# Inverse-step units in the transform's last slots, a penalty placed later, and fewer constant products

## The chip, the cores and the metric

The kernel runs on one core of a Trainium2 chip. The metric is the device time of one execution in microseconds, taken as the median of several runs. Before the change it is 1426.28 us (three runs, 1420.32 to 1427.12 us).

## The reference

A Fourier filter along the sequence, and then a layer of eight experts with a fixed capacity. Each token goes to its best expert that still has room, the tokens being served in the order of their largest scores; 19,968 tokens, 2,496 places per expert.

```python
def _attn_ref(x, filt_r, filt_i):              # x: (8, 2496, 256)
    X = np.fft.rfft(x, axis=1)
    Y = X * (filt_r + 1j * filt_i)[None]
    return np.fft.irfft(Y, n=x.shape[1], axis=1).astype(np.float32)

def _moe_ref(x, w_gate, w1, w2):               # N, D, E, F = 19968, 256, 8, 1024
    logits = x @ w_gate
    order = np.argsort(-logits.flatten())
    for idx in order:
        tok, e = int(idx) // E, int(idx) % E
        if assigned[tok] >= 0 or counts[e] >= N // E:
            continue
        assigned[tok] = e
        counts[e] += 1
    for e in range(E):
        h = np.maximum(x[assigned == e] @ w1[e], 0.0)
        out[assigned == e] = h @ w2[e]
```

## The kernel before, in words

**Transform.** The class Fft works through the eight batches in slots, ten to a batch: a list of events in run(), each with a slot and a priority, is sorted and emitted in that order, and a scheduler then arranges the instructions of each engine. Per batch there are two forward steps (s1, s2), the filter, transposes (tr, line 246) and a first inverse step (inv1, line 291), whose result goes to the tensor zd in DRAM. The scores of the gate are taken in the frequency domain: gate products (line 257), a copy of their sums (line 259), a transpose back (trv, line 282), and inverse steps of their own (v1, v2, v3, lines 326 to 353).

**Last inverse step.** It is cut into 40 units, five to a batch (inv2, lines 390 to 413). A unit loads a tile z from zd (line 375, SP's queue), multiplies it by the constant cD on TensorE in up to three products (line 408), copies each product from PSUM (line 409, ScalarE here) and stores the rows to the tensor xs (line 412). A unit has five columns and three products (512, 512 and 256 wide), the fifth of each batch two columns and one product. The units of the last six batches are the list rest, 30 of them, numbered from 0. The table FILL (line 28) gives the slots, counted from the end of the transform, in which its first units run, each followed by the load of the unit 15 places on, into a buffer that comes free. The others run behind the transform, and the last seven of them store from SP's queue.

**Routing.** The class Route serves the experts in eight phases. Phase 0 finds, in eleven rounds, a threshold for the expert that fills up first: VectorE compares the scores with candidates (Gm, line 587), TensorE counts (line 595, then line 608 over the partitions), VectorE picks the next candidates. At the end it has the members; places() turns them into row numbers, chunk by chunk of 512 rows (lines 787 to 810; xid at line 803 are the rows to gather). Line 755 adds a penalty to the scores of the full expert before phase 1 looks at them again (reduction at line 672, equality and multiplication at 674 and 676, reduction at 678, the assignment matrix A at 682).

**The seam.** Behind the transform, TensorE's order is written by hand: the generator after() hands out the rest of the units product by product, and the class Pump places the steps of the routing between them, by a clock of its own to which each piece of TensorE work adds its length. When the row numbers of the first chunk stand in the program, the remaining units are emitted, and after them 36 constant products (line 1051), whose result nobody reads. POOL then issues the load of the first expert's first weight (line 834) behind the copy of the last unit, four gathers of rows from xs (line 853), and the load of the second weight. The gathers wait for the row numbers and for all stores to xs.

**Experts.** The class Ffn transposes the gathered rows (turn, line 867; copies at 870 and 871), multiplies by the first weight (line 888) and by the second (lines 946 and 948), adds the halves on POOL (line 959) and scatters rows to the output (line 960). The weights are split into a high and a low part (split, copy on ScalarE at line 846, difference on VectorE at line 847). The routing of the next phase runs beside each expert, its counts in TensorE's queue between the expert's products.

Of the kernel before, what the change touches and what calls it, by code (L numbers as in the profile page):

```python
# [9 lines left out]
AF, OP, AX = mybir.ActivationFunctionType, mybir.AluOpType, mybir.AxisListType  # L10
# [6 lines left out]
S = B * G  # L17
# [7 lines left out]
ORD, TF = (1, 0, 0, 1), (3, 5)  # L25
ORD2 = [(0, f) for f in range(6)] + [(1, f) for f in range(4)] + [(0, 6), (0, 7)] + [(1, f) for f in range(4, 8)]
I1, EZ = 5, 0.8
FILL = (-1.5, 0.0, 1.5)
V1, V1D, V2, V3, VP, I2, AC = 8, 0.5, 3, 2, -1, 5, 6.5
NP, NZ, MZ, NXO, ZB, NH = 6, 4, 8, 4, 2, 10  # L30

# [89 lines left out]
class Fft:  # L121
# [293 lines left out]
    def run(s, cp, wp, xp, ps, freed, prep, rest):  # L415
# [51 lines left out]
        for u in rest[NZ:NZ+3]:  # L467
            at(10*B - min(3, I2 - 5.6), 9, s.load_z, *u)
        for k, o in enumerate(FILL):
            at(10*B + o, 5, s.inv2, *rest[k])  # L470
# [17 lines left out]
class Route:  # L488
# [176 lines left out]
    def phase(s, ph):  # L665

        nc = s.nc
# [29 lines left out]
        if ph < 7:  # L697
# [22 lines left out]
            with s.tc.issue_after(x.ins):  # L720
                expert()
                nc.vector.tensor_tensor_scan(cum, s.one[:117], eqm, 0.0, op0=OP.mult, op1=OP.add)
                pen = v("pen", [128, 8])
# [28 lines left out]
        if ph == 7:  # L752
            return
        if ph == 0:
            nc.vector.tensor_tensor(s.lg, s.lg, pen[:117].unsqueeze(1).to_broadcast([117, S, 8]), op=OP.add)
        for e in range(8 if ph else 0):
            nc.scalar.activation(s.lg[:, :, e], s.lg[:, :, e], AF.Identity, bias=pen[:117, e:e+1], scale=1.0)  # L757
        with s.tc.issue_after(s.last):
# [212 lines left out]
def emit(tc, i, out):  # L971
    nc = tc.nc
    with ExitStack() as st:
# [29 lines left out]
        def after():  # L1003
            nonlocal W
            q = 5
            for k in range(len(FILL), len(rest)):
                if k == 3 + NZ + MZ:
# [34 lines left out]
        with tc.manual_schedule(engines={mybir.EngineType.PE}):  # L1042
            while (0, 0) not in pump.tags:
                pump.feed(0.1)
                c = next(units, None)
                pump.feed(c if c else 0.8)
            for c in units:
                pass
            p = ps.tile([128, 512], F32, name="rest", tag="b", bufs=2)
            for _ in range(36):  # L1050
                nc.tensor.matmul(p, R.ones16[:117], R.iota, start=True, stop=True)

        zst.close()
# [135 lines left out]
```

## Time and profile before

| | |
|---|---|
| median of three runs | 1426.28 us |
| profiled execution | 1427.79 us |
| its span | 1426.0 us |
| TensorE busy | 1375.7 us, 96% |
| VectorE busy | 938.6 us, 66% |
| ScalarE busy | 715.8 us, 50% |
| POOL busy | 656.2 us, 46% |
| granted TensorE clock, mean | 0.987 |

The rows below come from this one profiled execution. PE is TensorE, DVE is VectorE, ACT is ScalarE, SP is the engine that only issues transfers. Times count from the start of the span. In a timeline a row is a start, a length, the engine and the line, with the number of records (one fp32 product is two records) and, in brackets, how long the engine sat idle before it and what ended that. Products are pipelined, so that the lengths of neighbours overlap.

### The profile page before, as it was taken

Reading aid. Unit: us, or ns where it says so; the run is one execution under the profiler, and the core shown is the slowest. Engines: PE = TensorE matmul, PEld = TensorE weight load, DVE = VectorE, ACT = ScalarE, POOL = GpSimd, SP = SyncE. Lnnn points to the kernel's source line nnn. Section 1 sums busy time; section 2 is a strip of 40 time slices with the busy share of each in tenths; the row PEclk is TensorE's granted clock in tenths of the full one; section 3 lists DMA queues with packets and bytes.
Section 4 is the critical chain, followed back from the end, with each engine's and each line's share of the span. In section 5 each row is a group of like instructions: output and inputs, shape, how many; then the busy total and the mean of one; then the engine's idle time right before and its main releaser. Section 6 shows DMA issues by size and latency. Waiting matters only on the chain.

```text
span 1426.0 us, 24833 instructions
## 1 busy us (share of the span) xinstructions
PE 1375.7 (96%) x9139; PEld 1142.4 (80%) x9139; DVE 938.6 (66%) x2575; ACT 715.8 (50%) x1644; POOL 656.2 (46%) x724
## 2 busy tenths in 40 slices
PE   8999999998988999999999999999999999999998
PEld 7999998776547788877887877787788788888887
DVE  6776766584686797668668768877867845333231
ACT  6777776444553464354436435534533645433332
POOL 6344443241025556554554653646536454445423
PEclk9999999998989999999999999999999999999999
DMA  9455556878961122121112112112101321111100
GB/s 357 152 166 159 159 154 174 245 266 272 345 253 56 33 96 62 32 85 49 51 36 90 54 45 84 52 43 95 45 27 54 131 71 47 41 47 54 40 23 28
DMA packets 55389, 152.37 MB, mean 107 GB/s; under 512 B 9356, under 2 KB 29964, under 8 KB 51172
## 3 DMA queue, kind: packets, MB, share of 16 engines
q0 software_dynamic: 17552, 57.72, 12.3%
q1 hardware_dynamic: 11357, 53.88, 10.4%
q10 hardware_dynamic: 26359, 39.19, 9.2%
q8 instruction: 72, 1.18, 0.3%
q14 instruction: 49, 0.40, 0.1%
HBM read 87.08 MB, written 63.70 MB: 106 GB/s over the span
## 4 chain that ended last, share of the span: by engine, by line
PE 58%; DVE 7%; ACT 2%; issue 2%; DMA 0%; POOL 0%; POOLq 0%; DVEq 0%; ACTq 0%
PE pz L888 26%; PE py L946 18%; PE py L948 9%; PE ptr L867 2%; PE rt L595 2%; DVE hl L902 1%; ACT lg L757 1%; PE py L938 1%; PE rt L795 1%; DVE OH L789 1%; DVE Gm L587 1%; ACT junka L800 1%; DVE X L605 0%; DVE z L871 0%; DMA xg<-xs,xid 0%
## 5 line engine op out<-in xcount | busy, mean ns | idle before, releaser
L946 PE MATMUL py<-w,hl 128*128 128x512 f32 x1216 | 336.4, 397 | 3.1 <-ACT y L958 3.1
L894 ACT ACTIVATE hl<-pz 128x512 fp32r<-128x512 f32 (+1 forms) x320 | 187.7, 588 | 222.2 <-PE pz L888 193.0
L959 POOL TENSOR_TENSOR y<-y 128x256 f32<-128x256 f32 x152 | 128.9, 850 | 309.0 <-ACT y L958 308.1
L888 PE MATMUL pz<-xo,w0h 128*128 128x512 f32 (+1 forms) x640 | 259.6, 406 | 8.7 <-DVE z L871 3.2
L888 PE MATMUL pz<-xo,w0l 128*128 128x512 f32 (+1 forms) x640 | 254.9, 398 | 0.0
L902 DVE SCALAR_TENSOR_TENSOR hl<-pz,hl 128x512 fp32r<-128x512 f32 x233 | 159.1, 686 | 123.0 <-ACT hl L894 110.3
L946 PEld LDWEIGHTS py<-w,hl 128*128 128x128 f32 x1216 | 210.3, 189 | 31.3 <-ACT y L958 3.5
L853 POOL DMA_INDIRECT xg<-xs,xid x160 | 167.0, 1044 | 107.3 <-issue 35.7
L958 ACT COPY y<-py 128x512 f32<-128x512 f32 x152 | 88.7, 586 | 248.3 <-PE py L948 178.2
L948 PEld LDWEIGHTS py<-w,hl 128*128 128x128 f32 x1216 | 185.6, 188 | 24.7 <-DVE hl L902 0.7
L948 PE MATMUL py<-w,hl 128*128 128x256 f32 x1216 | 200.1, 284 | 0.3 <-DVE hl L902 0.2
L888 PE MATMUL pz<-z,w0h 128*128 128x512 f32 (+1 forms) x640 | 196.6, 388 | 0.0
L960 POOL DMA_INDIRECT out<-y,oid x160 | 171.4, 1071 | 45.5 <-POOL y L959 34.7
L888 PEld LDWEIGHTS pz<-xo,w0h 128*128 128x128 f32 x640 | 121.8, 190 | 32.0 <-DVE z L871 3.9
L888 PEld LDWEIGHTS pz<-z,w0h 128*128 128x128 f32 x640 | 121.4, 190 | 21.7 <-DVE z L871 0.2
L219 ACT COPY Y<-p 64x240 f32<-64x240 f32 (+1 forms) x304 | 116.2, 382 | 41.6 <-PE p L212 20.3
L888 PEld LDWEIGHTS pz<-xo,w0l 128*128 128x128 f32 x640 | 122.3, 191 | 15.5
L235 POOL TENSOR_TENSOR P<-P 128x256 f32<-128x256 f32 x80 | 58.7, 734 | 163.2 <-DVE P L233 162.1
L587 DVE TENSOR_TENSOR Gm<-M,thr 117x1232 bf16<-117x1232 f32 (+2 forms) x80 | 104.4, 1315 | 0.2
L212 PE MATMUL p<-cS,xr 117*128 117x120 f32 x688 | 97.5, 281 | 2.3 <-DMA xr<-xl 2.3
L212 PEld LDWEIGHTS p<-cS,xr 117*128 117x128 f32 x688 | 89.3, 198 | 5.3 <-DMA xr<-xl 2.5
L227 PE MATMUL p<-cW,Y 128*128 128x128 f32 x640 | 88.1, 277 | 1.8 <-ACT Y L219 1.8
(233 smaller groups left out, 2228.7 us busy)
## 6 DMA issues: line engine op xcount, KB each, us to landing
zd<-zt ACTq DMA_DIRECT2D x80, 256.0 KB
xr<-xl SPq DMA_DIRECT2D x6, 1536.0 KB
z<-zd SPq DMA_DIRECT2D x14, 640.0 KB
xr<-xl SPq DMA_DIRECT2D x7, 1216.0 KB
xs<-xo ACTq DMA_DIRECT2D x13, 600.0 KB
xr<-zd SPq DMA_DIRECT2D x8, 640.0 KB
xs<-xr ACTq DMA_DIRECT2D x8, 600.0 KB
xs<-Y ACTq DMA_DIRECT2D x6, 600.0 KB
```

Source lines behind the costliest of these rows:

```text
L212: nc.tensor.matmul(p[:, q-q0, :120], s.xr[b][:117, q], s.cS1, start=True, stop=True)
L219: x = (nc.vector.tensor_copy if dve else nc.scalar.copy)(dst, src)
L587: nc.vector.tensor_tensor(Gm[:, s0:s1, :m], s.M[:, s0:s1].unsqueeze(2).to_broadcast([117, s1 - s0, m]), thr[:117].unsqueeze(1).to_broadcas ...
L853: s.lastg = s.nc.gpsimd.indirect_dma_start(out=xg[:n], out_offset=None, in_=s.xs, in_offset=bass.IndirectOffsetOnAxis(ap=ids[0][:n, t:t+1] ...
L888: nc.tensor.matmul(p[:, :n], w[:, sl], x[:, k, :n], start=m == 0, stop=m == 5)
L894: s.lasta = nc.scalar.activation(h[:, :n], p[:, :n], AF.Relu).ins
L902: nc.vector.scalar_tensor_tensor(l[:, :n], p[:, :n], 0.0, h[:, :n].bitcast(F32), op0=OP.max, op1=OP.subtract)
L946: nc.tensor.matmul(pp, hs[g][f][:, hi], w2[:, :, 256*f:256*f+256], start=m == 0, stop=False, skip_group_check=True)
L948: nc.tensor.matmul(pp[:, f % 2], hs[g][f][:, lo], w2h[:, 256*f:256*f+256], start=False, stop=m > 13, skip_group_check=True)
L958: s.lasta = nc.scalar.copy(yy, pp).ins
L959: nc.gpsimd.tensor_tensor(y, y, yy[:, 1], op=OP.add)
L960: st = nc.gpsimd.indirect_dma_start(out=out_rows, out_offset=bass.IndirectOffsetOnAxis(ap=ids[1][:w, 4*g+t:4*g+t+1], axis=0), in_=y[:w], i ...
```

## The change

It has three parts. FILL gets five entries instead of three: the first five units of the list run in the last slots of the transform, units 3 and 4 being new there, with the loads of units 18 and 19. The penalty of phase 0 is to be issued behind the instruction that Route.last names, the first chunk's row numbers. Of the constant products there are 32 instead of 36.

```diff
@@ -25,7 +25,7 @@
-FILL = (-1.5, 0.0, 1.5)
+FILL = (-3.0, -1.9, -0.8, 0.3, 1.4)
@@ -752,7 +752,8 @@
         if ph == 0:
-            nc.vector.tensor_tensor(s.lg, s.lg, pen[:117].unsqueeze(1).to_broadcast([117, S, 8]), op=OP.add)
+            with s.tc.issue_after(s.last):
+                nc.vector.tensor_tensor(s.lg, s.lg, pen[:117].unsqueeze(1).to_broadcast([117, S, 8]), op=OP.add)
@@ -1047,7 +1048,7 @@
             p = ps.tile([128, 512], F32, name="rest", tag="b", bufs=2)
-            for _ in range(36):
+            for _ in range(32):
                 nc.tensor.matmul(p, R.ones16[:117], R.iota, start=True, stop=True)
```

From line 755 on, a line of the changed kernel has a number that is higher by one. How instructions stand in the two kernels at three places:

TensorE at the end of the transform, the last batch's transposes (L246), gate products (L257) and transform of the gate's sums (L326). Before, the first unit in the list starts behind the first transpose of sums:

```order
L246 MATMUL pa<-fid,P 128x128 x8
...
L257 MATMUL pv<-P,gate 32x128 x8
L282 MATMUL pv<-fid,vs 128x128
L408 MATMUL pv<-z,cD 120x512 x2
L408 MATMUL pv<-z,cD 120x256
L326 MATMUL pv<-cEh,Vh 8x128
L326 MATMUL pv<-cEl,Vh 8x128
```

Now:

```order
L246 MATMUL pa<-fid,P 128x128 x4
L408 MATMUL pv<-z,cD 120x512
...
L408 MATMUL pv<-z,cD 120x512
L408 MATMUL pv<-z,cD 120x256
L246 MATMUL pa<-fid,P 128x128 x4
L257 MATMUL pv<-P,gate 32x128 x8
L408 MATMUL pv<-z,cD 120x512 x2
L408 MATMUL pv<-z,cD 120x256
L282 MATMUL pv<-fid,vs 128x128
```

A unit stands ahead of the gate products and another between these and the transpose of their sums; the fifth has its one product between the last two groups of transposes, and behind that the last chain (gate products, transpose of sums, L326) has no unit in it, as before.

TensorE behind the last sums of phase 0 (L735), up to the constant products. Before:

```order
L408 MATMUL pv<-z,cD 120x512 x2
L408 MATMUL pv<-z,cD 120x256
L408 MATMUL pv<-z,cD 120x512 x2
L408 MATMUL pv<-z,cD 120x256
L408 MATMUL pv<-z,cD 120x512
L795 LDWEIGHTS OH
L795 MATMUL rt<-tab,OH 128x180
...
L408 MATMUL pv<-z,cD 120x512
L408 MATMUL pv<-z,cD 120x256
L408 MATMUL pv<-z,cD 120x512
```

Now:

```order
L408 MATMUL pv<-z,cD 120x512
L408 MATMUL pv<-z,cD 120x256
L408 MATMUL pv<-z,cD 120x512 x2
L408 MATMUL pv<-z,cD 120x256
L408 MATMUL pv<-z,cD 120x512
L796 LDWEIGHTS OH
L796 MATMUL rt<-tab,OH 128x180
...
L1052 LDWEIGHTS ones
L1052 MATMUL rest<-iota,ones 128x512
```

Ten products stood there and six do; the two pairs of row-number products now follow each other, and the constant products follow them.

VectorE at the first expert's weights: splits of the first weight (w0l) and the second (w), row numbers of the second chunk (xid), and the steps of phase 1. Before:

```order
L847 TENSOR_TENSOR w0l<-wr_5012,w0h 128x512
L678 TENSOR_REDUCE ar<-tmp 117x176
L847 TENSOR_TENSOR w0l<-wr_5012,w0h 128x512 x2
...
L847 TENSOR_TENSOR w_5016<-wr_5013,w_5016 128x512
L682 TENSOR_TENSOR A<-ar,row 117x1232
L847 TENSOR_TENSOR w_5016<-wr_5013,w_5016 128x512
L803 SCALAR_TENSOR_TENSOR xid<-ex,js 128x4
```

Now:

```order
L848 TENSOR_TENSOR w_5031<-wr_5028,w_5031 128x512
L804 SCALAR_TENSOR_TENSOR xid<-ex,js 128x4
...
L676 TENSOR_TENSOR tmp<-tmp,val_3582 117x1408
L903 SCALAR_TENSOR_TENSOR hl<-pz,hl 128x512
...
L678 TENSOR_REDUCE ar<-tmp 117x176
L903 SCALAR_TENSOR_TENSOR hl<-pz,hl 128x512
...
L682 TENSOR_TENSOR A<-ar,row 117x1232
```

Phase 1's multiplication, reduction and matrix A have gone behind all splits of both weights, with two evictions of the first expert's products (L903) between them.

## Rows read from the trace of the kernel before

**Rows 1.** Windows by stage: stretch, then busy us and records of each engine.

```profile
core 0: us, PE busy (x) PEld busy (x) DVE busy (x) ACT busy (x) POOL busy (x), PEclk, DMA share, GB/s
311.00:329.00 18.00, 15.55 (x145) 10.10 (x144) 9.66 (x15) 10.36 (x24) 1.57 (x3) 0.99 0.99 367
329.00:339.00 10.00, 8.90 (x54) 8.19 (x51) 2.61 (x9) 2.88 (x5) 1.47 (x2) 0.51 0.54 198
...
345.00:404.00 59.00, 58.50 (x273) 32.07 (x272) 40.84 (x149) 33.65 (x72) 1.70 (x1) 1.00 0.95 344
...
412.00:420.00 8.00, 2.63 (x9) 1.31 (x9) 6.48 (x17) 4.93 (x15) 4.42 (x5) 0.62 0.50 165
```

**Rows 2.** Timeline of PE at the end of the transform: start us, length us.

```profile
326.44 0.65 PE L257 MATMUL pv<-P,gate 128*32 128x128 f32 x16 [0.73 <-ACT P L248]
327.86 0.33 PE L282 MATMUL pv<-fid,vs 128*128 128x128 f32 x1 [0.78 <-ACT vs L259]
...
338.69 0.34 PE L595 MATMUL rt<-A,Gm 117*48 117x128 bf16 x2
```

**Rows 3.** Timeline of PE, from the last sums to the first expert.

```profile
395.95 5.39 PE L408 MATMUL pv<-z,cD 120*120 120x512 f32 x14
...
401.34 2.34 PE L408 MATMUL pv<-z,cD 120*120 120x512 f32 x6
...
403.67 7.93 PE L1051 MATMUL rest<-iota,ones 117*128 117x512 f16 x36
...
415.38 1.12 PE L867 MATMUL ptr<-id,xg 128*128 128x128 f32 x4 [3.46 <-DMA xg<-xs,xid]
...
419.87 0.80 PE L888 MATMUL pz<-xo,w0h 128*128 128x512 f32 x1 [1.06 <-ACT xo L870]
```

**Rows 4.** Timeline of DVE: the penalty and the first row numbers.

```profile
395.98 1.62 DVE L755 TENSOR_TENSOR lg<-lg,pen 117x1408 f32<-117x1408 f32 x1
...
405.82 0.16 DVE L803 SCALAR_TENSOR_TENSOR xid<-ex,js 128x4 int32<-128x4 f32 x1
```

**Rows 5.** Timeline of POOL: first weight load and first gather.

```profile
405.58 1.06 POOL L834 DMA_INDIRECT wr<-w1l,widx  x1 [0.69 <-issue]
411.59 1.00 POOL L853 DMA_INDIRECT xg<-xs,xid  x1 [4.95 <-DVE r L774]
```

**Rows 6.** Timeline of SP: the last stores to xs.

```profile
393.57 12.29 SPq L412 DMA_DIRECT2D xs<-xo  x7
```

**Rows 7.** DMA issues by line: count, KB each.

```profile
z<-zd SPq DMA_DIRECT2D x14, 640.0 KB
...
xs<-xo ACTq DMA_DIRECT2D x13, 600.0 KB
```

**Rows 8.** Timelines of ACT and DVE at the first expert's weights.

```profile
422.28 2.18 ACT L846 CAST w<-wr 128x512 fp32r<-128x512 f32 x4 [1.54 <-DMA wr<-moe_w,widx]
...
412.17 0.89 DVE L676 TENSOR_TENSOR tmp<-tmp,val 117x1408 bf16<-117x1408 bf16 x1
...
416.25 1.61 DVE L678 TENSOR_REDUCE ar<-tmp 117x176 f32<-117x1408 bf16 x1
...
423.60 1.44 DVE L682 TENSOR_TENSOR A<-ar,row 117x1232 bf16<-117x1232 f32 x1
```

**Rows 9.** Timeline of PE at the first count of phase 1.

```profile
425.09 0.72 PE L595 MATMUL rt<-A,Gm 117*48 117x112 bf16 x11 [0.22 <-DVE A L682]
...
429.06 0.19 PE L608 MATMUL rt<-X,ones 128*128 128x21 f16 x1 [1.66 <-DVE X L605]
429.79 0.41 PE L867 MATMUL ptr<-id,xg 128*128 128x128 f32 x2 [0.55 <-DMA xg<-xs,xid]
430.95 0.68 PE L867 MATMUL ptr<-id,xg 128*128 128x128 f32 x2 [0.75 <-DMA xg<-xs,xid]
431.29 0.78 PE L888 MATMUL pz<-xo,w0h 128*128 128x512 f32 x1
```

**Rows 10.** Costliest groups of the page: busy us, mean ns of one.

```profile
L902 DVE SCALAR_TENSOR_TENSOR hl<-pz,hl 128x512 fp32r<-128x512 f32 x233 | 159.1, 686 | 123.0 <-ACT hl L894 110.3
```

## The prediction

> **What bounds the kernel now.** I read the windows by stage first, then TensorE's timeline through the seam between transform and experts, then the engines that it waits for there. Three things are to be seen.
>
> In the transform's last slots, 311 to 329 us, TensorE is busy for 15.55 of 18 us, so 2.45 us are idle; the DMA engines are full (share 0.99). In the next 10 us it runs at a granted clock of 0.51, which is the lower of its two levels, 1.2 GHz, and the DMA share falls to 0.54 [rows 1]. The clock fell behind two waits on copies, 0.73 us before the gate products and 0.78 us before the transpose of their sums [rows 2].
>
> From 345 to 404 us TensorE is full (58.50 of 59 us), and so are the DMA engines (0.95 at 344 GB/s) [rows 1]. What stands there in TensorE's queue is what the stretch lasts: the units' products with the counts of phase 0 between them. The last unit product ends at 403.68 us, the constant products fill 403.67 to 411.6 us, and then TensorE idles for 3.46 us until the first gathered rows are there [rows 3]. The gather is not waiting for its row numbers: they are written at 405.98 us [rows 4], and POOL issues the gather at 411.59 us [rows 5], which is when the stores of the inverse transform are through; SP issued the last of these by 405.86 us [rows 6]. So the end of the seam is set by the stores, these by the last unit and by the bytes ahead of them.
>
> Behind it comes a second bound, VectorE. The first count of phase 1 starts at 425.09 us, after 0.22 us of waiting for the assignment matrix A; then TensorE waits 1.66 us for X and 0.55 and 0.75 us for gathered rows, and goes on with products at 431.29 us [rows 9].
>
> From there on TensorE is the bound to the end, and its order and POOL's are the same in both kernels, row for row behind the constant products. What the seam gains or loses is thus carried to the end unchanged.
>
> **The change, part by part.**
>
> *Two more units in the slots.* Unit 3 has three products, unit 4 (two columns instead of five) has one. Each product is two records, so eight records leave the stretch after 339 us. The last 20 records of such products took 5.39 and 2.34 us [rows 3], 0.387 us each: eight are 3.1 us. The same 3.1 us are added between 311 and 329 us. What is gained is the idle time that they fill. Of the 2.45 us [rows 1], 0.78 us is a copy in a chain of the last batch [rows 2] that has no unit beside it in the new order either; of the other 1.7 us I count 1.4 as filled. Bounds: nothing filled, 0; all filled and the lower clock of the next stretch gone as well, 8.90 us of busy time [rows 1] at half its length, 4.4 more. I take 1.4, since the two copies that the clock fell behind are still there. The last count of round 0 (338.69 us [rows 2]) then comes 1.7 us later, and the last unit product 1.4 us earlier.
>
> *Their transfers.* Each unit brings one load for a later unit on SP's queue and one store on ScalarE's: 640 and 600 KB [rows 7], two fifths of that for unit 4, together 1.4 x 1,240 = 1,736 KB. They move out of the full stretch and into 329 to 339 us, where the share was 0.54. On SP the two loads now stand ahead of those of the Vh and Vl buffers, which wait for a later step anyway, so nothing behind them starves. At 344 GB/s the bytes are worth 5.0 us. So the stores are through between 1.4 us (by the last product) and 5.0 us (by the bytes) earlier. I take 4.0: nearer to the bytes, since 5.7 us passed between the last store's issue [rows 6] and the gather [rows 5] with the engines at 0.95.
> POOL issues the first weight load at 405.58 us [rows 5], while those stores are under way; it follows the copy of the last unit, so it comes forward with it.
> Here the Trainium skill speaks against the change: DMA: Bandwidth & Descriptors, section "Issuing engines are not separate DMA queues", says that transfers started by SP, ScalarE and POOL run interleaved on the same 16 engines. By that the weight load would keep its place among the last stores, the gather would gain the 1.4 us alone, and the sum below would be 1.6 us slower. No row here separates the two kinds of transfer.
>
> ScalarE gets the four copies of these products in the slots; it is busy for 10.36 of the 18 us [rows 1], so they lie beside TensorE's work.
>
> *The penalty behind the first row numbers.* It takes 1.62 us on VectorE ahead of the sums that the row numbers need [rows 4]. The row numbers come up to 1.6 us sooner, but they are 5.6 us ahead of the gather now; price nothing. The cover is the stores; were it gone, the gain would be 1.6. Ahead of phase 1's first reduction the 1.62 us come back.
>
> *Four constant products fewer.* 7.93 us for 36 [rows 3] is 0.22 each, 0.9 us. Behind them TensorE is idle for 3.46 us [rows 3]: price nothing. Their purpose is the clock, which is down at 0.62 in 412 to 420 us with all 36 [rows 1].
>
> *What the scheduler does with it on VectorE.* This is not in the diff. Before, the multiplication for phase 1 (0.89 us), its reduction (1.61) and the matrix A (1.44) stand between the splits of the first expert's weights, and A ends at 425.04 us [rows 8]. Now all three stand behind the last split of the second weight and the second row numbers. ScalarE's four copies end at 424.46 us [rows 8]. From there: the last split and two evictions that stand between, 0.69 us each by the row of the same shape [rows 10], 2.1; the three, 3.9; small ones, 0.6 by estimate. A then ends at 431.1 us instead of 425.04, 6.0 us later against the gather. TensorE's queue is in order, so the count and everything behind it wait. But the 2.96 us of waits behind it [rows 9] are for things that are there by then. Net 3.0. Bounds: 0, if the splits come sooner than I put them and VectorE makes it up; 6.0, if the later waits stay, for example because the products between them run at the lower clock.
>
> *Sum.* -4.0 for the gather and +3.0 for A: -1.0 us. The profiled execution took 1427.79 us, its span 1426.0; it becomes 1426.8. The median of the three runs shown is 1.5 us below it, so the forecast is **1425.3 us**. A measurement of this kernel can tell about 0.5% from no change, 7.1 us: no difference that can be told.
>
> **The rivals.**
>
> *The clock holds.* If the denser slots keep TensorE at 2.4 GHz past 329 us, up to 4.4 us more are saved before the rounds, though VectorE's preparation between then limits it. The bytes let the gather follow to about 5.5 us. For it: the idle time ahead of the fall is what the units fill. Against: the two waits on copies stay. With A's 3.0 it is 1423.8; where VectorE also hides A, 1420.8.
> The Trainium skill, TensorE: Matmul & The Clock Gate, section "What's actually happening", says that the clock is throttled by default and that activity releases it; that would favour this rival, and the fall at 329 us agrees with it.
>
> *Slower: A costs all of it.* The place is the first count of phase 1. If TensorE is at the lower clock behind the long wait, the products up to 431 us take as much more as the old waits give back, and the 6.0 us stand; with a gather only 1.4 us sooner that is 4.6 us slower, 1430.9. It decides from the point where A ends over 4 us later against the gather. For it: the clock fell behind waits of 0.73 and 0.78 us [rows 2], far shorter than this one.
>
> *The stores do not follow.* The bytes are not what holds them; the gather is 1.4 us sooner, A costs 3.0: 1.6 us slower, 1427.9. For it: the weight load starts right behind the last unit in both kernels. Against: the share of 0.95. The Trainium skill's page DMA: Bandwidth & Descriptors is on its side.
>
> *The change does not do what it says.* The order shows that it does: five units stand ahead, and the penalty behind the row numbers.
>
> **How the numbers follow.** My forecast 0.45, the clock 0.15, A in full 0.2, the stores 0.2. Their times lie between 1420.8 and 1430.9; the runs before lie between 1420.32 and 1427.12 themselves, so I add about 1 us at either end: 1419.5 to 1431.5. Over 0.5% faster is below 1419.2: only the first rival with more than I worked out, 0.13. Slower by as much is above 1433.4: A in full with no gain at the gather, 0.07. The rest, 0.8, is within.
>
> **What would show it.** Right: idle time in 311 to 329 us falls; the constant products start about 1.4 us sooner; the gather is issued near 407.6 us; the wait before the first count of phase 1 is some 6 us long, and the three waits behind it are gone. Wrong: a granted clock near 1 in the ten us behind the slots; a gather that stays near 410 us; or a count of phase 1 that waits for nothing.

## The result and the profile after

The changed kernel takes 1436.72 us (median of 13 runs, 1430.49 to 1441.3), the kernel before, beside it, 1425.97 us: a ratio of **1.0079, 95% interval 1.0061 to 1.0096**. It is slower by 0.8%, more than the 0.5% that can be told from no change. The forecast was 1425.3 us with a range up to 1431.5.

The ratio of e9 below leaves out one of its 12 executions, which took 3118.39 us.

The profiled execution took 1435.77 us. Windows of after: two that answer to [rows 1] by the clock of the span, the same two shifted by the 6.94 us that are explained below, and two at the first expert:

```profile
core 0: us, PE busy (x) PEld busy (x) DVE busy (x) ACT busy (x) POOL busy (x), PEclk, DMA share, GB/s
311.00:329.00 18.00, 12.01 (x103) 7.33 (x104) 2.79 (x6) 7.76 (x20) 0.00 (x0) 0.95 0.97 386
329.00:339.00 10.00, 8.90 (x56) 8.05 (x53) 3.04 (x11) 2.88 (x5) 1.52 (x2) 0.57 0.39 122
...
304.06:322.06 18.00, 15.94 (x124) 9.64 (x123) 9.47 (x14) 9.87 (x23) 1.57 (x3) 1.00 0.99 364
322.06:332.06 10.00, 5.36 (x49) 3.79 (x48) 0.19 (x1) 3.07 (x7) 0.00 (x0) 0.77 0.87 318
...
424.00:432.00 8.00, 0.82 (x10) 0.85 (x11) 7.00 (x16) 1.52 (x6) 5.36 (x4) 0.65 0.17 49
432.00:436.00 4.00, 4.00 (x16) 2.94 (x14) 1.32 (x7) 0.60 (x1) 0.00 (x0) 0.50 0.11 33
```

In 311 to 329 us TensorE is idle for 6.0 us, not for less than 2.45, but this compares different work. In the stretch that answers to it by the count below, 304.06 to 322.06 us, it is idle for 2.06 us, hardly less than before, and the loss lies in the ten us behind that, 4.64 us idle. In 424 to 432 us it does nearly nothing, and behind that its granted clock is 0.50, the lower level.

**Where to count from.** Read by the clock of the span, the seam seems no loss: the constant products start at 402.41 us instead of 403.67. That is an accident of the two executions. The first product of the filter step starts at 21.64 us in the execution of before and at 17.02 in that of after, though nothing ahead of it was changed; in the 14 executions of this study it lies between 16.91 and 21.64. From there to the last filter product the two take 288.38 and 286.06 us, the 14 between 285.4 and 288.8, also with nothing changed. Together this is 6.94 us between the two clocks. TensorE's timelines, before:

```profile
21.64 2.05 PE L227 MATMUL p<-cW,Y 128*128 128x128 f32 x16 [1.52 <-ACT Y L219]
...
310.02 1.05 PE L227 MATMUL p<-cW,Y 128*128 128x128 f32 x8
...
328.46 0.23 PE L326 MATMUL pv<-cEh,Vh 128*8 128x128 f32 x1 [0.28 <-ACT Vh L285]
330.59 2.95 PE L342 MATMUL pv<-fid,Y 8*120 8x8 f32 x22 [0.67 <-ACT Y L328]
...
495.79 0.20 PE L608 MATMUL rt<-X,ones 128*128 128x63 f16 x1
```

and after, with the rows that answer to [rows 2, 3, 9]:

```profile
17.02 2.05 PE L227 MATMUL p<-cW,Y 128*128 128x128 f32 x16 [1.51 <-ACT Y L219]
...
303.08 1.05 PE L227 MATMUL p<-cW,Y 128*128 128x128 f32 x8
...
324.49 0.33 PE L282 MATMUL pv<-fid,vs 128*128 128x128 f32 x1 [0.39 <-ACT vs L259]
328.41 0.28 PE L326 MATMUL pv<-cEh,Vh 128*8 128x128 f32 x1 [3.59 <-ACT Vh L285]
330.54 2.95 PE L342 MATMUL pv<-fid,Y 8*120 8x8 f32 x22 [0.67 <-ACT Y L328]
...
402.41 7.07 PE L1052 MATMUL rest<-iota,ones 117*128 117x512 f16 x32
412.62 0.65 PE L868 MATMUL ptr<-id,xg 128*128 128x128 f32 x2 [2.83 <-DMA xg<-xs,xid]
...
419.06 0.79 PE L889 MATMUL pz<-xo,w0h 128*128 128x512 f32 x1 [0.67 <-ACT xo L871]
...
431.18 1.19 PE L595 MATMUL rt<-A,Gm 117*48 117x112 bf16 x11 [7.29 <-DVE A L682]
...
498.96 0.20 PE L608 MATMUL rt<-X,ones 128*128 128x63 f16 x1
```

So I count from the last filter product (the last L227, 310.02 and 303.08 us), which stands ahead of everything that the two orders do differently. Us from there, by the rows above, [rows 3] and the same rows of the experiments (each of these has its own runs of before beside it for the ratio, with medians between 1422.85 and 1426.19 us):

| kernel | L342 | constant products | first expert product | last count of phase 1 (L608) | ratio |
|---|---|---|---|---|---|
| before | 20.57 | 93.65 | 109.85 | 185.77 | 1 |
| after | 27.46 | 99.33 | 115.98 | 195.88 | 1.0079 |
| e1 five units only | 27.29 | 101.55 | 116.54 | 195.66 | 1.0052 |
| e2 penalty only | 20.10 | 94.01 | 110.81 | 189.28 | 1.0021 |
| e3 32 products only | 20.09 | 93.28 | 109.81 | 184.94 | 0.9984 |
| e4 after, A ahead of z | 27.11 | 99.17 | 116.78 | 193.77 | 1.0051 |
| e5 after, unit 4 late | 22.98 | 94.81 | 110.95 | 190.04 | 1.0029 |
| e6 after, A ahead | 27.84 | 99.71 | 114.89 | 190.84 | 1.0038 |
| e7 both repairs | 22.98 | 95.57 | 110.88 | 186.89 | 1.0015 |
| e8 = e3, A ahead | 20.09 | 93.20 | 109.53 | 184.49 | 0.9997 |
| e9 = e2, A ahead | 20.10 | 93.72 | 110.80 | 186.52 | 1.0001 |
| e10 52 products | 20.10 | 94.07 | 109.79 | 185.91 | 0.9995 |
| e11 five units, all repaired | 22.97 | 96.33 | 110.27 | 185.38 | 0.9999 |
| e12 52 products, rows early | 20.10 | 93.05 | 111.47 | 182.98 | 0.9976 |

By this count after is 6.9 us later at L342, of which 3.1 are the four products that moved there and should come back in the rounds; 5.7 later at the constant products, 6.1 at the first expert product, and 10.1 at the end of phase 1's counts. The medians differ by 10.7. Each row is one execution; the six experiments and before that have three units in the slots agree to 0.5 us at L342 and 1.0 us at the constant products.

**First loss: ScalarE's queue.** ScalarE's timeline of after at the last transposes:

```profile
319.11 0.32 ACTq L412 DMA_DIRECT2D xs<-xo  x1
...
324.17 0.27 ACT L259 COPY vs<-pv 128x128 f32<-128x128 f32 x1
327.69 0.59 ACT L409 COPY xo<-pv 120x512 f32<-120x512 f32 x1 [3.25 <-DMA xs<-xo]
328.17 0.19 ACT L285 CAST Vh<-pv 128x32 fp32r<-128x32 f32 x1
```

The copy of unit 4 waits 3.25 us for its buffer. In the slots the units take the two buffers xo in turn (line 400), so unit 4 has that of unit 2, whose store was issued at 319.11 us into a stretch with a DMA share of 0.97 and let go of it only at 327.69. Vh, the cast of the gate's sums, stands behind that copy in ScalarE's order, and TensorE waits for Vh for 3.59 us at L326.

**Second loss: VectorE's order.** VectorE's timeline of after, the rows that answer to [rows 4, 8]:

```profile
405.21 0.16 DVE L804 SCALAR_TENSOR_TENSOR xid<-ex,js 128x4 int32<-128x4 f32 x1
...
405.46 1.62 DVE L756 TENSOR_TENSOR lg<-lg,pen 117x1408 f32<-117x1408 f32 x1
...
424.55 0.68 DVE L848 TENSOR_TENSOR w<-wr,w 128x512 fp32r<-128x512 f32 x1
...
425.40 0.88 DVE L676 TENSOR_TENSOR tmp<-tmp,val 117x1408 bf16<-117x1408 bf16 x1
...
427.02 1.61 DVE L678 TENSOR_REDUCE ar<-tmp 117x176 f32<-117x1408 bf16 x1
...
429.59 1.44 DVE L682 TENSOR_TENSOR A<-ar,row 117x1232 bf16<-117x1232 f32 x1
```

A ends at 431.03 us behind the last split, and the first count waits 7.29 us for it, against 0.22 before [rows 9].

### The profile page after: what moved, and what is told of

Same layout as the page of the kernel before. It is cut to its first block, busy times and chain, and to the rows that moved or that the text cites. A ratio compares the mean times of both kernels' runs of the same rounds, so it can differ in the third digit from the quotient of the medians.

```text
span 1434.0 us, 24825 instructions
## 1 busy us (share of the span) xinstructions
PE 1376.1 (96%) x9135; PEld 1141.3 (80%) x9135; DVE 940.6 (66%) x2575; ACT 716.7 (50%) x1644; POOL 658.2 (46%) x724
## 4 chain that ended last, share of the span: by engine, by line
PE 80%; DVE 9%; ACT 3%; DMA 2%; issue 2%; POOL 1%; ACTq 0%; POOLq 0%; DVEq 0%
PE pz L889 26%; PE py L947 18%; PE py L949 9%; PE pv L408 4%; PE p L227 4%; PE p L212 4%; PE pa L291 4%; PE rt L595 2%; PE ptr L868 2%; PE pa L246 2%; DVE Gm L587 2%; PE pv L257 1%; DVE hl L903 1%; ACT lg L758 1%; DMA xs<-xo 1%
## 5 line engine op out<-in xcount | busy, mean ns | idle before, releaser
L903 DVE SCALAR_TENSOR_TENSOR hl<-pz,hl 128x512 fp32r<-128x512 f32 x233 | 159.4, 687 | 123.5 <-ACT hl L895 111.1
L854 POOL DMA_INDIRECT xg<-xs,xid x160 | 168.8, 1055 | 109.5 <-issue 36.4
L587 DVE TENSOR_TENSOR Gm<-M,thr 117x1232 bf16<-117x1232 f32 (+2 forms) x80 | 105.4, 1328 | 0.2
L227 PE MATMUL p<-cW,Y 128*128 128x128 f32 x640 | 88.1, 277 | 1.9 <-ACT Y L219 1.8
```

Of the source, the lines that this page charges most:

```text
L227: nc.tensor.matmul(p[:, k], s.Y1[b][:, 4*g+k, dh*128:dh*128+128], s.cW[:, 4*g+k], start=True, stop=True)
L587: nc.vector.tensor_tensor(Gm[:, s0:s1, :m], s.M[:, s0:s1].unsqueeze(2).to_broadcast([117, s1 - s0, m]), thr[:117].unsqueeze(1).to_broadcas ...
L854: s.lastg = s.nc.gpsimd.indirect_dma_start(out=xg[:n], out_offset=None, in_=s.xs, in_offset=bass.IndirectOffsetOnAxis(ap=ids[0][:n, t:t+1] ...
L903: nc.vector.scalar_tensor_tensor(l[:, :n], p[:, :n], 0.0, h[:, :n].bitcast(F32), op0=OP.max, op1=OP.subtract)
```

## The experiments

**e1, e2, e3: one part of the change each.** Each is the kernel before with one of the three edits of the diff.

*e1, five units.* 

> Only the FILL table is changed (five units in the slots); the penalty stands in its old place and there are 36 constant products. On VectorE the matrix A of phase 1 stands behind all four splits of the second weight here too, with one eviction of the first expert's products between. Theory 'A late' (the matrix A behind the second weight's splits makes TensorE wait at the first count of phase 1 and what follows carries it): a wait of 5 us or more at that count, and about 1433 us or more, nearly all of the change's 10 us. Theory 'penalty' (the 1.62 us on VectorE moved in front of phase 1 cost the time): no slower than before, 1423 to 1427 us. Theory 'ScalarE' (the fifth unit's copy waits for its buffer ahead of Vh): a wait of 3 us or more at L326 near 325 us, as with the whole change.

*e2, the penalty.* 

> Only the penalty is moved behind the first row numbers; three units in the slots, 36 constant products. A stands behind all four splits of the second weight and two evictions. Theory 'A late': a long wait (4 us or more) at the first count of phase 1 with the gather as before, so 4 us or more slower: 1430 or more. Theory 'penalty': slower by some 2 to 10 us, and the first fill alone not. Rival 'slots' (the loss comes from the units in the transform's last slots): 1426, the same as before.

*e3, 32 products.* 

> Only 32 constant products instead of 36. A stands between the second and the third split of the second weight, much as before. Theory 'A late': no wait at the first count of phase 1 beyond 1 us, and the time of before, 1424 to 1428. Rival 'clock' (four products fewer let the clock fall earlier or longer in front of the first expert): slower by 1 to 3 us, and a lower granted clock in 404 to 431 us.

| part | ratio, 95% | wait at L326 | wait at the first count |
|---|---|---|---|
| e1 five units | 1.0052, 1.0033 to 1.0070 | 3.44 us | 7.58 us |
| e2 penalty | 1.0021, 1.0006 to 1.0037 | 0.3 us | 5.27 us |
| e3 32 products | 0.9984, 0.9970 to 0.9998 | 0.3 us | 1.94 us |

The five units alone bring both waits. The penalty alone brings the one at the count. So it is not one part that puts A late. That the scheduler sorts VectorE anew because each edit gives it other durations is my reading; the orders differ, but no run shows why. I had expected the five units to cost nearly all of the 10 us; they cost two thirds. Of the penalty I had expected 4 us or more; it costs 3. Of e3 I had expected a wait of at most 1 us at the count; it is 1.94. But e3, where A is least late of the three, is not slower, against the rival "clock". The three parts add up to 1.0057, the whole change has 1.0079; the intervals are too wide to tell these two apart.

**e4, e6: A ahead, in the whole change.** In e4 one half of the transposed rows and the splits of the second weight are held behind A:

```diff
+        last = W.turn(0, 0, 0)
+        with tc.issue_after(R.lastA):
+            last = W.turn(0, 0, 1)
+        with tc.issue_after(last), tc.issue_after(R.lastA):
             while split:
                 W.split(*split.pop(0))
```

> The whole change, and two edges on VectorE: the second half of the first expert's transposed rows and the splits of the second weight are issued behind the matrix A of phase 1. Nothing else moves ahead of the first expert. Theory 'A late': A ends near 422 us, the first count of phase 1 waits under 1 us, products go on 3 to 5 us earlier than in the changed kernel, and the time comes down from 1436.7 to 1430 or less; if all of the loss hangs on it, to 1423 to 1426. Rival 'later stages' (most of the loss arises behind 450 us, from the clock after waits that are the same in both kernels): it stays at 1432 or more, though the wait at the count is gone.

It recovers part: 1.0051 (1.0035 to 1.0068). The wait at the count is gone, but one of 5.66 us for z has taken its place. A still ended at 430.61 us. By the count from the filter that is 123.87, only 4.1 sooner than in after (127.95), where before has 115.02: ahead of it in VectorE's order stood the second row numbers, and these waited 3.43 us for sums on ScalarE. The edge had named the wrong instruction. In e6 the splits of the first weight, both halves of the rows and the second row numbers are held behind A:

```diff
-        with tc.issue_after(f.lastst):
+        with tc.issue_after(f.lastst), tc.issue_after(R.lastA):
             while len(split) > 4:
...
+                if (ph, ch) == (0, 1):
+                    hold.enter_context(s.tc.issue_after(s.lastA))
                 nc.vector.tensor_scalar(js[:, ts], js[:, ts], 0.5, S / 2, op0=OP.mult, op1=OP.add)
```

> The whole change, with edges on VectorE that put phase 1's multiplication, reduction and the matrix A ahead of the splits of the first expert's first weight and of the second chunk's row numbers. Theory 'A late': A ends before 419 us counted as in the changed kernel (some 10 us behind the first gather's issue), the wait of 7.3 us at the first count is gone; the splits behind it delay the first expert's products by 1 to 2 us; 3 to 5 us come back, a ratio of 1.0045 to 1.006. Rival 'the wait only moves' (what comes behind the count is late anyway: second row numbers, gather, half clock): at most 1 us comes back, 1.007 or more.

1.0038 (1.0024 to 1.0051), 5.0 us sooner at the end of phase 1's counts than after. TensorE's timeline of e6 at the first expert:

```profile
420.29 0.80 PE L892 MATMUL pz<-xo,w0h 128*128 128x512 f32 x1 [0.68 <-ACT xo L874]
423.18 0.79 PE L892 MATMUL pz<-xo,w0l 128*128 128x512 f32 x1 [2.10 <-DVE w0l L851]
...
426.19 1.22 PE L892 MATMUL pz<-z,w0h 128*128 128x512 f32 x2 [1.36 <-DVE z L875]
...
429.59 0.72 PE L595 MATMUL rt<-A,Gm 117*48 117x112 bf16 x11
```

The count waits for nothing; 2.10 and 1.36 us are paid for the splits that now come later. A ended at 421.35 us rather than before 419, 10.3 us behind the first gather's issue, which is the distance expected.

**e5, e7: unit 4 behind the chain.** Its slot is 2.95 instead of 1.4, so that its product and copy stand behind the last sums:

```diff
-FILL = (-3.0, -1.9, -0.8, 0.3, 1.4)
+FILL = (-3.0, -1.9, -0.8, 0.3, 2.95)
```

> The whole change, but the fifth unit of the slots has its product and its copy behind the last sums of the scores (its slot is 2.95 instead of 1.4), so that ScalarE's Vh copy no longer stands behind a copy that waits for its buffer. Theory 'ScalarE': TensorE's wait at the last L326, 3.3 to 3.6 us in the changed kernel, falls below 1 us, L342 comes about 3.3 us sooner, counted from the last product of the filter step (L227), and the time falls by 2.5 to 3.5 us against the changed kernel: a ratio to before of 1.0055 instead of 1.0079. Rival 'stores' (the transfers in the full stretch hold the next step whatever stands in ScalarE's order): the wait moves to another instruction and the ratio stays above 1.007.

e7 has this and the edges of e6. 

> Both of the two repairs at once in the changed kernel. If the two places make up the whole loss and their prices add: 6 to 8.5 us back, a ratio of 1.0018 to 1.0035. If the rest of the loss (about 2 us in the rounds of phase 0, where units are missing that covered VectorE's candidates) is right too, not below 1.001. Rival 'clock or later stages': no lower than 1.005.

e5 gives 1.0029 (1.0016 to 1.0041). TensorE's timeline of e5:

```profile
305.99 1.05 PE L227 MATMUL p<-cW,Y 128*128 128x128 f32 x8
...
327.31 0.23 PE L326 MATMUL pv<-cEh,Vh 128*8 128x128 f32 x1 [0.28 <-ACT Vh L285]
...
428.96 1.19 PE L595 MATMUL rt<-A,Gm 117*48 117x112 bf16 x11 [6.53 <-DVE A L682]
```

The wait for Vh is 0.28 us and L342 stands at 22.98 instead of 27.46 (0.8 of it because unit 4's product is now behind). The ratio fell further than I had expected. The constant products come 4.5 us sooner than in after, so the rounds of phase 0 have not lengthened again. Their first two waits for candidates (L595 near 345 us, for Gm) are 1.56 and 1.44 us in after, 1.22 and 0.37 before, 0.27 and 0.37 in e5; e11, with the same slots, has one of 1.46 again, so how much of this belongs to the repair is open. e7 gives 1.0015 (1.0000 to 1.0031), 9.0 of the 10.1 us by the table. The two places make up nearly the whole loss.

**e8, e9, e11: what the parts are worth with A in its place.** The edges of e6 on e3, on e2, and on e3 with the five units of e5.

*e8.* 

> Only 32 constant products, with the edges that put A ahead of the first weight's splits; three units, penalty in its old place. Theory 'A late': the 1.9 us of waiting at the first count in the kernel with 32 products goes, and 1 to 3 us are gained against it: a ratio to before of 0.996 to 0.998. Rival 'the wait only moves': the same as with 32 products alone, 0.9984, or slower, since the splits of the first weight come later.

*e9.* 

> The penalty moved behind the first row numbers, nothing else of the change (three units, 36 constant products), with the edges that put the matrix A ahead of the splits of the first weight. If the penalty's move costs only through the place that the scheduler then gives A: the 5.3 us of waiting at the first count are gone, and the ratio falls from 1.0021 to that of the kernel with 32 products and A ahead, 0.9997 or less. If the 1.62 us on VectorE ahead of phase 1 are the price themselves: it stays at 1.001 to 1.002.

*e11.* 

> Five units in the slots with the fifth behind the last sums (ScalarE's wait repaired), the old place of the penalty, 32 constant products, A ahead of the first weight's splits: what the fuller slots are worth by themselves, beside the kernel with the same edges and three units (ratio 0.9997). By the working of the prediction the slots' idle time is filled and the gather is sooner: 1 to 4 us faster than that one, 0.997 to 0.999. If no idle time is filled, because each wait there is a chain of copies that no unit shortens: no faster, 0.9995 to 1.0015.

e8 is a miss: 0.9997 (0.9984 to 1.0011). Its count no longer waits, but X and the second rows do, 2.36 us and 0.59 and 0.50; where A is only 2 us late, moving it forward gains nothing. e9 gives 1.0001 (0.9989 to 1.0014) for 1.0021, not quite the 0.9997: the wait at the count is gone, and most of the price of the penalty's move with it. Something is left: in e2 and e9 the first expert product stands at 110.8 us in the table, in before, e3, e8 and e10 at 109.5 to 109.9 (more on this at the gather, below). e11 gives 0.9999 (0.9982 to 1.0015): the fuller slots by themselves are worth nothing that can be told, beside e8. TensorE's timeline of e11 shows why:

```profile
312.41 0.23 PE L326 MATMUL pv<-cEh,Vh 128*8 128x128 f32 x1 [0.50 <-ACT Vh L285]
...
317.81 0.65 PE L257 MATMUL pv<-P,gate 128*32 128x128 f32 x16 [0.68 <-ACT Y L248]
...
318.84 2.41 PE L408 MATMUL pv<-z,cD 120*120 120x512 f32 x6 [0.38 <-ACT vs L259]
...
321.86 0.23 PE L326 MATMUL pv<-cEh,Vh 128*8 128x128 f32 x1 [0.50 <-DVE Vl L286]
...
324.76 0.33 PE L282 MATMUL pv<-fid,vs 128*128 128x128 f32 x1 [0.57 <-ACT vs L259]
...
325.36 0.23 PE L326 MATMUL pv<-cEh,Vh 128*8 128x128 f32 x1 [0.27 <-ACT Vh L285]
```

With 0.66 at L342 the waits from the last filter product to there are 3.56 us; before, by the same rows, they are 3.13, and in after 6.72. Each ends with a copy that the next instruction in TensorE's order waits for, and units that stand elsewhere don't cover it.

**e10, e12: the clock, and a better order.** e10 is the kernel before with 52 constant products. 

> The kernel before with 52 constant products instead of 36, so that they last until about the time when the first gathered rows are there (16 more at 0.22 us are 3.5 us). VectorE's order is not quite the same: A stands ahead of the second weight's splits, the second row numbers behind them. Rival 'the clock is the price' (half the clock in front of and within the first expert's products costs what the seam loses): the clock stays at 1 until 415 us or later, the first products come 1 to 2 us sooner, ratio 0.996 to 0.998. If the waits of the transposes on rows, of some 0.5 us each, bring the clock down all the same, or VectorE sets the pace there: 0.999 to 1.001, or up to 1.002 if the products outlast the wait.

A window of e10, and then the window of before that answers to it by the count:

```profile
412.00:420.00 8.00, 5.63 (x17) 3.59 (x18) 7.81 (x17) 4.83 (x15) 0.74 (x1) 0.79 0.44 147
```

```profile
417.36:425.36 8.00, 6.26 (x22) 4.18 (x21) 6.47 (x12) 6.36 (x20) 0.28 (x1) 0.57 0.38 138
```

The clock is granted at 0.79 there, for 0.57, and the first product starts 5.4 us sooner by the span's clock, but no sooner counted from the filter. The ratio is 0.9995 (0.9979 to 1.0011). At the first count nothing of what the clock gave is left: it starts at 115.30 us by the count, before at 115.07. Behind the first four products TensorE waited 0.80 us for z, and the next products took 0.63 us instead of 0.40. Behind the count it waited for the second gather. TensorE's timeline of e10:

```profile
416.44 1.22 PE L888 MATMUL pz<-z,w0h 128*128 128x512 f32 x2 [0.80 <-DVE z L871]
...
426.11 1.24 PE L867 MATMUL ptr<-id,xg 128*128 128x128 f32 x4 [2.93 <-DMA xg<-xs,xid]
```

That gather stood behind row numbers that stood behind the four splits of the second weight. So e12 puts the sums and row numbers ahead of these splits:

```diff
-        with tc.issue_after(last):
+        with tc.issue_after(last), tc.issue_after(R.rows1), tc.issue_after(R.lastj):
             while split:
                 W.split(*split.pop(0))
```

> The kernel before with 52 constant products, and edges that put the second chunk's row numbers (on ScalarE the four sums that they need, on VectorE xid) ahead of the splits of the second weight. In the kernel with 52 products alone TensorE waited 2.93 us for the second gather's rows, issued at 422.65 us, 0.3 us behind row numbers that stood behind four splits. Theory 'order on VectorE and ScalarE sets the seam': the second gather is issued some 4 us sooner, the 2.93 us go, and 2 to 3 us are gained: a ratio to before of 0.9975 to 0.9985, faster than both kernels. Rival 'the wait only moves' (the splits of the second weight, now later, hold the first products with it, or the lower clock takes it back): 0.999 to 1.0005.

e12 gives **0.9976 (0.9956 to 0.9997)**, faster than both kernels, by the amount expected, though the interval ends close to 1. The second gather is issued 3.7 us sooner by the count, and TensorE does not wait for it. POOL's timelines at the second gather, e10 and then e12:

```profile
422.65 0.94 POOL L853 DMA_INDIRECT xg<-xs,xid  x1 [9.91 <-DVE t L809]
```

```profile
418.42 0.94 POOL L855 DMA_INDIRECT xg<-xs,xid  x1 [4.47 <-DVE t L811]
```

The window of e12 that answers to that of e10:

```profile
412.00:420.00 8.00, 6.07 (x18) 4.11 (x17) 7.10 (x19) 4.73 (x14) 2.92 (x4) 0.57 0.45 160
```

Its clock there is 0.57, lower than in e10, so the gain is not the clock's. Between e10 and e12 only the order differs, and by the table e12 is 2.9 us sooner at the end of phase 1's counts, although its first expert product stands 1.7 us later. Their two intervals overlap, and the same edges with 36 constant products were not tried.

## Why the prediction was wrong

*Two more units: "of the other 1.7 us I count 1.4 as filled".* This step failed. Nothing was filled (up to L342 the waits are 3.56 us in e11 and 3.13 before), and a wait of 3.59 us came. I had placed the four copies on ScalarE by its busy time ("they lie beside TensorE's work") and not by its order: what counts is what stands behind a copy, here Vh, and what the copy itself waits for, here a buffer. I looked at what the transfers starve on SP's queue only. The bounds of this term had no loss in them, though nothing excluded one. Forecast 1.4 us sooner at the last unit product; measured 5.5 later there by the count (99.19 us against 93.66), 3.3 of them at L326 and the rest mostly in the rounds of phase 0.

*The gather, -4.0.* Mis-sized. It is issued 6.58 us behind the last unit product (402.27 us to 408.85) instead of 7.91 [rows 3, 5], 1.3 sooner, where the sum wanted 2.6. POOL's row of after:

```profile
408.85 0.96 POOL L854 DMA_INDIRECT xg<-xs,xid  x1 [3.95 <-DMA xs<-xo]
410.12 2.67 POOL L854 DMA_INDIRECT xg<-xs,xid  x1 [0.30 <-issue]
```

The weight load starts right behind the last unit, as the rival "the stores do not follow" had it. The Trainium skill, DMA: Bandwidth & Descriptors, section "Issuing engines are not separate DMA queues", says that transfers started by different engines interleave on the same 16 DMA engines; by that, as I applied it in the prediction, the gather would have gained nothing against the last unit product. The 1.3 us lie halfway between that and the bytes' 2.6, and no row shows the transfers interleaved.

And the first expert product is not sooner: it starts 10.21 us behind the first gather, before 8.28. POOL took 7.1 us for the four gathers instead of 4.8, the second one 2.67 us (above) instead of 0.98 (here before, POOL):

```profile
412.90 0.98 POOL L853 DMA_INDIRECT xg<-xs,xid  x1 [0.30 <-issue]
```

In after VectorE compares the scores for phase 1 beside that gather, before it had done so ahead of the first one (408.80 to 410.42 us):

```profile
409.72 1.62 DVE L674 TENSOR_TENSOR tmp<-lg,M 117x1408 bf16<-117x1408 f32 x1
```

All nine kernels with five units or the later penalty, e2 and e9 among them, have one of these four gathers at 1.46 us or more, and it overlaps with this step or the one right behind it on VectorE (L587); in the other five both end ahead of the first gather, and none is above 1.24. That one causes the other was not tested.

*A, 6.0 later and net 3.0.* The mechanism and its place were right: the count waits, and the three waits behind it are gone. From the end of ScalarE's copies (423.93 us) to the end of A I had counted 6.6 us, and it is 7.1. But against the gather A is 8.7 us later, not 6.0 (22.18 us behind it, before 13.45), since the copies themselves end 2.2 us later behind it. That I put the end of A at 431.1 us and it is 431.03 is luck: the two clocks stand 6.94 us apart. The net price was too small: 4.0 us from the first expert product to the end of phase 1's counts (75.92 before, 79.90 after). e6 takes all of it back (75.95), and between e5 and e7 it is 3.1 (79.09 and 76.01). The products behind the long wait run at the lower clock (0.50 in 432 to 436 us), as the rival "A costs all of it" said; I gave it 0.2.

*The penalty, nothing.* Untrue of the edit (e2): it is one of the two that move A. With A ahead (e9) the ratio shows no price, the table about 1 us at the first expert product. *Four products, nothing.* Within 0.2% (e3); the interval ends at 0.9998, and what gains there is not settled.

*The clock holds.* It did not (0.57 in 329 to 339 us, before 0.51). At another place it held for longer in e10, and that gained nothing.

*The signs.* One more sign of being right came true by luck: by the clock of the span the constant products start 1.26 us sooner, as forecast, in a kernel that is 10 us slower. I had tied it to a clock that differs from execution to execution.

*The sum.* For the -4.0 at the gather it was +4.2 us there by the count, and +6.1 at the first expert product, for the +3.0 of A +4.0: 10.1 us for -1.0. The range ended 5 us too low because both rivals that lost time took the first term as a gain.

What stays open: from the end of phase 1's counts to the last count of the last phase that has any, after took 606.4 us and before 603.2, the other kernels 600.5 to 604.0, with the same order. Of the 3.1 us between after and before, 2.2 lie at the one place that the last section shows. I have not tested whether after's 606.4 is more than chance.

## What to carry to other kernels

Work that is put into an engine's idle time has to be followed on every engine that it crosses: what stands behind its copy in that engine's order, and when the buffer that the copy needs comes free. Where a scheduler sorts an engine, an edit elsewhere can move a step that another engine waits for; compare the orders first, and pin the two or three steps that matter. And compare two executions from a common instruction just ahead of the change, not by the clock of the span.

## What was not expected of the hardware

Of 14 executions whose program is the same up to there, the first filter product started between 16.91 and 21.64 us.

The same wait was followed by the lower clock for different lengths of time. Near 770 us both kernels wait 2.03 us for z with the same order around it. The windows behind it, of before and then of after:

```profile
775.00:780.00 5.00, 5.00 (x25) 3.98 (x24) 5.00 (x19) 3.50 (x9) 0.26 (x1) 0.93 0.08 26
```

```profile
780.00:785.00 5.00, 5.00 (x14) 3.64 (x14) 3.85 (x15) 0.99 (x3) 0.00 (x0) 0.52 0.08 26
```

Before, the clock was back within 4 us of the wait's end; after, it was still at 0.52 in the stretch from 3 to 8 us behind it. In after a second, short wait stands between, which before does not have:

```profile
779.18 0.80 PE L889 MATMUL pz<-xo,w0h 128*128 128x512 f32 x1 [0.52 <-DVE hl L903]
```

From the end of the first wait to the products by the second weight it is 9.54 us in after and 7.34 in before. So what follows a wait that is the same in two kernels can differ by 2 us in one execution; how much of it is the clock and how much the second wait is not separated.
